# Block products for a second two-unit stage, and a new order of loads before it, in a fused linear-attention and bilinear-FFN kernel

## The chip, the core and the metric

The kernel runs on one core of a Trainium2 chip. The metric is the device time of one execution in microseconds (us), the median of 8 runs. An execution takes a little longer than the span of its instructions in the profile. Engines: TensorE (PE; its weight loads are PEld), VectorE (DVE), ScalarE (ACT), GpSimd (POOL) and SyncE (SP), which only issues DMAs. Each engine works through its own instructions in order.

## The reference

Four batches, eight heads, 768 positions, head size 64, in float32. In blocks of 64 positions, with a decay `lam` for each head:

```python
intra = einsum('bhic,bhjc->bhij', qb, kb) * Dmask     # lam**(i-j), lower triangle
out   = intra @ vb + (qb * lam_pow) @ kv_state
kv_state = lam**64 * kv_state + (kb * rev_pow).T @ vb
```

The heads are then laid side by side, x of 3072 x 512, and a bilinear FFN follows: `(x @ w_a) * (x @ w_b) @ w_out`, with `d_ff` = 1536.

## The kernel before, in words

**Units.** A unit is 128 positions of one batch with all heads: 24 units, six for each batch. For each unit the kernel scales q and k by powers of `lam` (`make_qs`, `make_ks`, line 240; k on VectorE for units below 10, else on GpSimd; q on GpSimd), transposes both (`piece_T`, line 271, on TensorE with a copy by ScalarE, for units 4 and 5; by a DMA from unit 6 on), computes scores (`scores`, 284), masks them on VectorE (`mask`, 307), updates the running state (`kv_update`, 362, copied on VectorE, 387), and forms the output from state and scores (`inter`, `intra`, matmuls of line 324), which ScalarE copies into the transposed x of the FFN (`evac_o`, 347).

**Stages.** The FFN works on groups of units, `GROUPS = (4, 2, 4, 4, 4, 4, 2)`. I call the groups stages 0 to 6. Units 0 to 3 are done by code of their own at the start (lines 720 to 786), and the attention of later units is threaded through the FFN of earlier ones. `PLAN` lists, for each stage, slots and pieces: P (scale q and k, load v, issue further loads), T (transpose), S (scores and masks), V (state), O2 (output of two units), TW (sums of weights), W (stores that were kept back). The FFN code calls `hook(slot)` at fixed places, and the pieces are issued there. An engine meets them in that order.

**Two forms of the FFN.** `ffn` (617) forms, for each of the 12 chunks of 128 hidden columns, a = x @ w_a and b = x @ w_b, four matmuls each (`half`, 430), and their product on VectorE (457). `ffn_seven` (484) gets the four blocks of a and b from seven block products instead of eight, in the manner of Strassen: it splits x in two halves of columns and two of rows, and uses sums of weights (`tw`, four per chunk pair, `w_sums`, 459 to 466, on VectorE) and sums of x (`xs`, `sums`, 468 to 480, on VectorE after the stage's last attention output). `step` (516) issues one product and what follows it: ScalarE takes snapshots of partial sums (513), VectorE and GpSimd add and multiply. The block `c11` is added by VectorE (532) for the chunks that `SUM_ON_VEC` names, else by GpSimd after another snapshot (535); one product is always GpSimd's (545). For a two-unit stage there are three blocks, 21 products of eight matmuls with 128 columns; for four units six blocks, 42 products of four matmuls with 256 columns. The hooks lie among the products:

```python
            if s % 7 == 1 and s < 42:
                hook(2 * (s // 7))
            if s % 7 == 4 and s < 35:
                hook(2 * (s // 7) + 1)
        hook(FC - 1)
```

With three blocks the loop ends after s = 25: slot 6 comes behind the 20th product, slot 7 at s = 25 behind no further one, slot 11 right after it, and the 21st product behind eight matmuls with w_out. `S_GROUPS` names the stages that use this form: 2 to 6. Stages 0 and 1 use `ffn`; stage 0 is special, since the weights arrive during it: it goes in steps of columns (`W_STEPS`), and all matmuls with w_out (line 608) come last, in 24 slots (12 to 35) of two matmuls each.

**Loads.** q and k go through SP's queue: eight loads of 256 KB for units 0 to 3, then two a unit (126). They are issued by `pump` (159), which lets at most three units run ahead. v (128 KB a unit, 256) and the weights (18 loads of 256 KB, 146 and 148) go through GpSimd's queue, which also converts them to bf16. Two holds keep the order. GpSimd first copies an element of a q chunk (`q_here`, 723), and so waits until it is there before it loads v. And SP copies an element of a w_out chunk into `landed` (163), and so waits for that chunk before it goes on: in `pending` (152), q and k of unit 4 wait for w_out's chunk 0, of unit 5 for chunk 3, all later for chunk 5.

Of the kernel before, what the change touches and what calls it, by code (L numbers as in the profile page):

```python
# [22 lines left out]
def _bc(ap, dims):  # L23
# [6 lines left out]
W_STEPS = ((0, 1), (2,), (3,), (4, 5))  # L30
# [7 lines left out]

S_GROUPS = (2, 3, 4, 5, 6)
SUM_ON_VEC = {2: (0, 1, 2, 3, 4), 3: (2, 3, 4), 4: (2, 3, 4), 5: (1, 2, 3, 4), 6: (0, 1, 2)}
PLAN = {
# [10 lines left out]
}  # L54
for _g, _u in ((2, 10), (3, 14), (4, 18)):
# [6 lines left out]
def kernel(  # L62
# [11 lines left out]
    nc = tc.nc  # L74
    B, H, S, D = q.shape
# [5 lines left out]
    NU = B * NB  # L81
    assert sum(GROUPS) == NU and GROUPS[0] == PACK
    KS = d_model // 128
    FC = d_ff // 128
# [45 lines left out]
    wb_sb = singles.tile([128, KS, d_ff], BF16, name="wb_sb")  # L130
    wo_sb = singles.tile([128, FC, d_model], BF16, name="wo_sb")
# [4 lines left out]
    w_off = [sum(W_CHUNKS[:i]) for i in range(len(W_CHUNKS) + 1)]  # L136
# [7 lines left out]
    def load_w(kind, c):  # L144
        if kind == "o":
            nc.gpsimd.dma_start(out=wo_sb[:, 2 * c:2 * c + 2, :], in_=wo_r[:, 2 * c:2 * c + 2, :])
        else:
            nc.gpsimd.dma_start(out=w_part(wa_sb if kind == "a" else wb_sb, c),
                                in_=w_part(wa_r if kind == "a" else wb_r, c))

    n0 = GROUPS[0]
    pending = [("after", 0), ("q", n0), ("k", n0), ("after", 3), ("q", n0 + 1), ("k", n0 + 1), ("after", 5)]
    for u in range(n0 + 2, NU):
        pending += [("q", u), ("k", u)]
    landed = singles.tile([1, 16], BF16, name="landed")
    q_here = singles.tile([128, 1], F32, name="q_here")
    used = {"u": 0}

    def pump():
        while pending:  # L160
            kind, c = pending[0]
            if kind == "after":
                nc.sync.dma_start(out=landed[:, c:c + 1], in_=wo_sb[0:1, 2 * c + 1, 0:1])
            elif c >= used["u"] + 3:
                return
            else:
                load_x(kind, c)
            pending.pop(0)
# [14 lines left out]
    x4 = {}  # L183
# [69 lines left out]
    def make_vb(u):  # L253
        b, nb = divmod(u, NB)
        vb = prep_pool.tile([128, H, D], BF16, name="vb", tag="vb", bufs=8)
        nc.gpsimd.dma_start(out=vb, in_=vr[b, nb])  # L256
        U.setdefault(u, {})["vb"] = vb
# [210 lines left out]
    def sums(u):  # L468
        g = next(i for i in range(len(GROUPS)) if g_u0[i] <= u < g_u0[i] + GROUPS[i])
        if g not in S_GROUPS or u != g_u0[g] + GROUPS[g] - 1:  # L470
            return
# [231 lines left out]
    def scores4(i, ups, ats):  # L703
        kqs = []
        for up, at in zip(ups, ats):
            kq = [ps_bank(f"kq{par}", [128, HP, 128], F32, at=at[par]) for par in range(2)]
            for uu in range(2):
                cols = slice((2 * up + uu) * BLK, (2 * up + uu + 1) * BLK)
                for j in range(2):
                    for par in range(2):  # L710
                        p = slice(64 * par, 64 * par + 64)
                        nc.tensor.matmul(kq[par][:, 2 * uu + j, :],
                                         lhsT=xT4["k"][p, 2 * i + j, cols],
                                         rhs=xT4["q"][p, 2 * i + j, cols],
                                         start=True, stop=True, skip_group_check=True)
            kqs.append(kq)
        for up, kq in zip(ups, kqs):
            ms4[i, up] = mask(kq, split=(i == 1 and up == 1))

    for u in range(n0):  # L720
        U[u] = dict(kn=kn4[:, u], qT=xT4["q"][:, :, u * BLK:(u + 1) * BLK],
                    m=lambda i, hp, u=u: ms4[hp // 2, u // 2][i][:, 2 * (u % 2) + hp % 2, :])
    nc.gpsimd.tensor_copy(q_here, x4["q", 3][:, 0, 0, 0:1])
    for u in range(n0):
        make_vb(u)
    for kind, c in (("a", 0), ("a", 1)):
# [23 lines left out]
    def kv_part(u, hps):  # L750
        for w in range(u + 1):
            kv_mms(sts[u], w, hps, w == 0)

    scores4(1, (0, 1), ((5, 2), (6, 0)))
    for cs in W_STEPS:
        for kind, c in [("a", c) for c in cs] + [("b", c) for c in cs]:
            if (kind, c) not in (("a", 0), ("a", 1)):
                load_w(kind, c)
    for c in range(FC // 2):
        load_w("o", c)  # L760
        if c in (3, 5):
            make_vb(n0 + (c - 3) // 2)
    for u in range(2):
        kv_part(u, (0, 1))
    for u in range(2):
# [21 lines left out]
    bank["held"].clear()  # L787
    used["u"] = n0
    pump()

    for g, n in enumerate(GROUPS):
# [62 lines left out]
```

## Time and profile before

| What | us |
|---|---|
| Median of 8 runs | 224.58 (224.04 to 225.17) |
| The profiled execution | 225.17 |
| Its span | 223.5 |
| Stage 0, a and b parts: from the first to w_out's first matmul | 18.48 to 39.45 |
| Stage 0, w_out with attention of units 4 and 5 between | 39.45 to 54.41 |
| Stage 1: a and b parts, attention of 6 to 9, w_out | 54.41 to 74.70 |
| Stages 2, 3, 4, 5 begin | 74.70, 108.66, 142.06, 175.50 |
| Stage 6 begins | 205.70 |

The page gives busy time for each engine, the span in 40 slices, and the costliest groups of instructions. Of the trace, the timeline lists instructions in order of time: start, duration, engine, line, operation, output and inputs, shape, count, and in square brackets how long the engine had been idle before and what ended that. A window gives busy time of each engine in a stretch, the granted clock of TensorE (1.00 is full), the busy share of the DMA engines, and GB/s.

### The profile page before, as it was taken

Reading aid. Unit: us, or ns where it says so; the run is one execution under the profiler, and the core shown is the slowest. Engines: PE = TensorE matmul, PEld = TensorE weight load, DVE = VectorE, ACT = ScalarE, POOL = GpSimd, SP = SyncE. Lnnn points to the kernel's source line nnn. Section 1 sums busy time; section 2 is a strip of 40 time slices with the busy share of each in tenths; the row PEclk is TensorE's granted clock in tenths of the full one; section 3 lists DMA queues with packets and bytes.
Section 4 is the critical chain, followed back from the end, with each engine's and each line's share of the span. In section 5 each row is a group of like instructions: output and inputs, shape, how many; then the busy total and the mean of one; then the engine's idle time right before and its main releaser. Section 6 shows DMA issues by size and latency. Waiting matters only on the chain.

```text
span 223.5 us, 5209 instructions
## 1 busy us (share of the span) xinstructions
PE 214.1 (96%) x2080; PEld 146.7 (66%) x2099; DVE 146.0 (65%) x250; ACT 99.8 (45%) x182; POOL 117.4 (53%) x131
## 2 busy tenths in 40 slices
PE   7898999989999999999999999999999999999994
PEld 2475444435874688754688754688754688745974
DVE  0991575975696788893678763578763598730760
ACT  2685224018432656324565424566424556332622
POOL 6689352058147569895178993178920144600240
PEclk9999999999999999999999999999999999999999
DMA  4999999989999999999960999500921200012102
GB/s 126 270 130 176 198 205 197 194 186 214 193 206 231 210 240 123 212 332 228 265 167 6 188 211 227 125 4 9 124 58 47 97 1 3 0 47 97 47 3 94
DMA packets 98605, 31.79 MB, mean 142 GB/s; under 512 B 86550, under 2 KB 95638, under 8 KB 98582
## 3 DMA queue, kind: packets, MB, share of 16 engines
q1 hardware_dynamic: 66390, 23.53, 46.5%
q0 software_dynamic: 31904, 7.87, 36.9%
q8 instruction: 16, 0.26, 0.5%
q10 hardware_dynamic: 288, 0.07, 0.1%
q14 instruction: 7, 0.06, 0.1%
HBM read 28.32 MB, written 6.29 MB: 155 GB/s over the span
## 4 chain that ended last, share of the span: by engine, by line
PE 59%; DMA 14%; POOL 13%; DVE 4%; issue 3%; ACT 3%; SPq 1%; POOLq 0%; ACTq 0%
PE op L608 22%; PE m_q L498 13%; DMA wb_sb<-in_moe_w_b_dram 8%; PE m_r L498 7%; POOL ab L545 5%; PE o_ps L324 4%; DMA vb<-in_v_dram 4%; POOL qk L240 3%; PE m_p L498 3%; PE kq L290 3%; DMA k<-in_k_dram 3%; PE a_ps L430 2%; PE b_ps L430 2%; POOL c L535 2%; POOL vb L256 2%
## 5 line engine op out<-in xcount | busy, mean ns | idle before, releaser
L608 PE MATMUL op<-wo_sb,ab 128*128 128x512 bf16 (+2 forms) x295 | 65.7, 362 | 2.0 <-issue 0.8
L545 POOL TENSOR_TENSOR ab<-c,c 128x512 bf16<-128x512 bf16 x27 | 31.4, 1166 | 33.8 <-DVE c L543 33.4
L498 PEld LDWEIGHTS <-tw 128*128 128x128 bf16 x480 | 43.2, 98 | 6.3 <-DVE xs L477 0.3
L608 PEld LDWEIGHTS <-ab 128*128 128x128 bf16 x312 | 27.6, 98 | 27.6 <-POOL ab L545 1.6
L307 DVE TENSOR_TENSOR m<-kq,lotri 128x512 bf16<-128x512 f32 x47 | 29.8, 684 | 6.6 <-PE kq L290 6.1
L498 PE MATMUL m_q<-xs,tw 128*128 128x256 bf16 (+1 forms) x240 | 32.4, 262 | 0.0
L603 ACT COPY o_sb<-op 128x512 f32<-128x512 f32 (+2 forms) x20 | 10.9, 544 | 44.3 <-PE op L608 44.3
L240 POOL TENSOR_TENSOR qk<-qf,lp_q 128x512 bf16<-128x512 f32 x20 | 21.0, 1051 | 17.3 <-DMA qf<-in_q_dram 17.3
L535 POOL TENSOR_TENSOR c<-s 128x512 bf16<-128x512 f32 x9 | 11.4, 1270 | 31.4 <-ACT s L513 31.4
L552 DVE TENSOR_TENSOR ab<-c,m_q 128x512 bf16<-128x512 f32 x27 | 18.6, 687 | 10.6 <-PE m_q L498 8.8
L498 PEld LDWEIGHTS <-wa_sb 128*128 128x128 bf16 x240 | 21.5, 98 | 2.9
L256 POOL DMA_DIRECT2D vb<-in_v_dram x24 | 22.3, 933 | 1.1 <-DMA wa_sb<-in_moe_w_a_dram 0.6
L457 DVE TENSOR_TENSOR ab<-a_sb,b_ps 128x512 bf16<-128x512 bf16 (+1 forms) x24 | 13.1, 551 | 14.1 <-PE b_ps L430 13.9
L513 ACT COPY s<-m_q 128x512 f32<-128x512 f32 x27 | 15.8, 587 | 14.4 <-PE m_q L498 14.1
L543 DVE TENSOR_TENSOR c<-u,m_r 128x512 f32<-128x512 f32 x27 | 18.4, 682 | 5.1 <-ACT u L513 3.2
L532 DVE TENSOR_TENSOR c<-s,m_p 128x512 bf16<-128x512 f32 x18 | 12.4, 687 | 11.1 <-PE m_p L498 11.0
L439 ACT CAST a_sb<-a_ps 128x512 bf16<-128x512 f32 (+1 forms) x24 | 11.4, 479 | 18.1 <-PE a_ps L430 18.1
L430 PE MATMUL a_ps<-xT,wa_sb 128*128 128x256 bf16 (+1 forms) x102 | 18.1, 312 | 1.0 <-DMA wa_sb<-in_moe_w_a_dram 0.9
L549 DVE TENSOR_TENSOR c<-s,m_q 128x512 f32<-128x512 f32 x27 | 18.5, 686 | 0.5
L513 ACT COPY s<-m_r 128x512 f32<-128x512 f32 x27 | 15.9, 588 | 6.5 <-PE m_r L498 6.5
L430 PE MATMUL b_ps<-xT,wb_sb 128*128 128x512 bf16 (+1 forms) x96 | 18.4, 326 | 0.1
L513 ACT COPY u<-m_q 128x512 f32<-128x512 f32 x27 | 16.0, 593 | 5.2 <-PE m_q L498 5.2
(81 smaller groups left out, 290.8 us busy)
## 6 DMA issues: line engine op xcount, KB each, us to landing
qf<-in_q_dram SPq DMA_DIRECT2D x20, 256.0 KB, 4.3
kf<-in_k_dram SPq DMA_DIRECT2D x20, 256.0 KB, 4.9
out_dram<-o_sb SPq DMA_DIRECT2D x17, 256.0 KB, 2.0
vb<-in_v_dram POOLq DMA_DIRECT2D x24, 128.0 KB, 4.8
wa_sb<-in_moe_w_a_dram POOLq DMA_DIRECT2D x6, 256.0 KB, 8.1
wb_sb<-in_moe_w_b_dram POOLq DMA_DIRECT2D x6, 256.0 KB, 8.6
wo_sb<-in_moe_w_out_dram POOLq DMA_DIRECT2D x6, 256.0 KB, 10.2
out_dram<-o_kept SPq DMA_DIRECT2D x6, 256.0 KB, 4.0
```

Source lines behind the costliest of these rows:

```text
L240: eng_of(eng).tensor_mul(dst.rearrange("p (c b) d -> p b c d", b=2), x[:].rearrange("p (b c) d -> p b c d", b=2), lp.rearrange("p (b c) o ...
L256: nc.gpsimd.dma_start(out=vb, in_=vr[b, nb])
L307: nc.vector.tensor_mul(m, kq[i], lotri_bc)
L430: nc.tensor.matmul(ps[:, lo:hi], lhsT=w_sb[:, s, f * 128:(f + 1) * 128], rhs=xT[:, s, lo:hi], start=(s == 0), stop=(s == KS - 1), skip_gro ...
L498: nc.tensor.matmul(ps[:, f, :], lhsT=w(k, f), rhs=x[:, k, :], start=(first and f == 0 and k == 0), stop=True, skip_group_check=True)
L513: nc.scalar.copy(t, ps)
L535: nc.gpsimd.tensor_add(d["c11"], d["s12"][:, 0], d["s12"][:, 1])
L543: nc.vector.tensor_add(c12, d["u2"], d["r"])
L545: nc.gpsimd.tensor_mul(ab[:, nf * i:nf * i + nf, 0:h], d["c11"], c12)
L549: nc.vector.tensor_add(d["c22"], d["s5"], d["q"])
L552: nc.vector.tensor_mul(ab[:, nf * i:nf * i + nf, h:2 * h], d["c22"], d["q"])
L608: nc.tensor.matmul(op[:, lo:hi], lhsT=ab[:, f, t * 128:(t + 1) * 128], rhs=wo_sb[:, f, lo:hi], start=(f == 0), stop=(f == FC - 1))
```

## The change

- Stage 1 uses `ffn_seven` as well (`S_GROUPS`), with all three `c11` on VectorE. The sums of x for it follow the output of units 4 and 5, which moves from slot 34 of stage 0 to slot 31, and with it all that comes before: units 4 and 5 are prepared at slots 15 and 20 instead of 23 and 27.
- The sums of weights, which stage 1 now needs, stand at slots 1, 3, 5, 7, 11 and 18 of stage 0 instead of 4 to 18.
- In stage 1 the attention of units 6 and 7 moves among the products: scores of 6 at slot 6, state of 6 and scores of 7 at slot 7, output of both at slot 11 as before. Some preparations move in stages 0, 1, 3 and 4.
- `SUM_ON_VEC`: in stages 2 to 5 the chunks whose `c11` VectorE adds are others (in 2 and 5 as many as before, in 3 and 4 three as before, now with the last one).
- `pending`: q and k of unit 4 wait for w_b's chunk 3, of unit 5 for w_out's chunk 0, of unit 6 for chunk 3, all later for chunk 5.
- `q_here` copies from q's chunk 1 instead of 3, so GpSimd loads v of units 0 to 3 sooner.
- Two chunks of w_b are issued ahead of a mask that GpSimd does for units 2 and 3, and v of unit 4 is loaded after w_out's chunk 2 instead of 3.

```diff
-S_GROUPS = (2, 3, 4, 5, 6)
-SUM_ON_VEC = {2: (0, 1, 2, 3, 4), 3: (2, 3, 4), 4: (2, 3, 4), 5: (1, 2, 3, 4), 6: (0, 1, 2)}
+S_GROUPS = (1, 2, 3, 4, 5, 6)
+SUM_ON_VEC = {1: (0, 1, 2), 2: (0, 1, 2, 3, 5), 3: (1, 3, 5), 4: (1, 3, 5), 5: (1, 2, 4, 5), 6: (0, 1, 2)}
 PLAN = {
-    0: [(0, "V", 3), (4, "TW", 0), (6, "TW", 1), (9, "TW", 2), (11, "TW", 3), (14, "TW", 4),
-        (18, "TW", 5), (23, "P", 4), (26, "T", 4), (27, "P", 5), (28, "S", 4), (30, "T", 5),
-        (31, "V", 4), (32, "S", 5), (34, "O2", (4, 5)), (35, "P", 6)],
-    1: [(1, "P", 7), (3, "P", 8), (6, "P", 9), (7, "S", 6), (8, "V", 6), (9, "S", 7), (11, "O2", (6, 7)),
+    0: [(0, "V", 3), (1, "TW", 0), (3, "TW", 1), (5, "TW", 2), (7, "TW", 3), (11, "TW", 4),
+        (15, "P", 4), (18, "TW", 5), (19, "T", 4), (20, "P", 5), (22, "S", 4), (25, "T", 5), (26, "V", 4),
+        (27, "P", 6), (28, "S", 5), (31, "O2", (4, 5)), (33, "P", 7)],
+    1: [(2, "P", 8), (4, "P", 9), (6, "S", 6), (7, "V", 6), (7, "S", 7), (11, "O2", (6, 7)),
         (12, "S", 8), (12, "V", 8), (13, "S", 9), (13, "P", 10), (14, "O2", (8, 9)), (15, "P", 11)],
...
-    3: [(6, "P", 18), (9, "P", 19), (13, "P", 20), (16, "P", 21)],
-    4: [(6, "P", 22), (9, "P", 23)],
+    3: [(4, "P", 18), (7, "P", 19), (13, "P", 20), (16, "P", 21)],
+    4: [(4, "P", 22), (7, "P", 23)],
...
-    pending = [("after", 0), ("q", n0), ("k", n0), ("after", 3), ("q", n0 + 1), ("k", n0 + 1), ("after", 5)]
-    for u in range(n0 + 2, NU):
+    pending = [("after", ("b", 3)), ("q", n0), ("k", n0), ("after", ("o", 0)), ("q", n0 + 1), ("k", n0 + 1),
+               ("after", ("o", 3)), ("q", n0 + 2), ("k", n0 + 2), ("after", ("o", 5))]
+    for u in range(n0 + 3, NU):
         pending += [("q", u), ("k", u)]
...
-                nc.sync.dma_start(out=landed[:, c:c + 1], in_=wo_sb[0:1, 2 * c + 1, 0:1])
+                i = used["gates"] = used["gates"] + 1
+                nc.sync.dma_start(out=landed[:, i:i + 1],
+                                  in_=wo_sb[0:1, 2 * c[1] + 1, 0:1] if c[0] == "o" else
+                                  wb_sb[0:1, 3, w_off[c[1]]:w_off[c[1]] + 1])
...
-    nc.gpsimd.tensor_copy(q_here, x4["q", 3][:, 0, 0, 0:1])
+    nc.gpsimd.tensor_copy(q_here, x4["q", 1][:, 0, 0, 0:1])
...
+    w_order = [(kind, c) for cs in W_STEPS for kind in "ab" for c in cs]
+    w_order += [("o", c) for c in range(FC // 2)]
+    for kind, c in w_order[2:4]:
+        load_w(kind, c)
     scores4(1, (0, 1), ((5, 2), (6, 0)))
-    for cs in W_STEPS:
-        for kind, c in [("a", c) for c in cs] + [("b", c) for c in cs]:
-            if (kind, c) not in (("a", 0), ("a", 1)):
-                load_w(kind, c)
-    for c in range(FC // 2):
-        load_w("o", c)
-        if c in (3, 5):
-            make_vb(n0 + (c - 3) // 2)
+    for kind, c in w_order[4:]:
+        load_w(kind, c)
+        if (kind, c) in (("o", 2), ("o", 5)):
+            make_vb(n0 + (c == 5))
```

More of the change, by code (lines that the diff above doesn't have):

```diff
@@ L156 @@
     q_here = singles.tile([128, 1], F32, name="q_here")
-    used = {"u": 0}
+    used = {"u": 0, "gates": 0}
     def pump():
```

## The prediction

> **What bounds the kernel now.** I read the page first, then the timeline of TensorE, then those of VectorE and GpSimd over the same microseconds, then the windows on the DMA.
>
> ```profile
> PE 214.1 (96%) x2080; PEld 146.7 (66%) x2099; DVE 146.0 (65%) x250; ACT 99.8 (45%) x182; POOL 117.4 (53%) x131
> ...
> PEclk9999999999999999999999999999999999999999
> ```
>
> TensorE is busy for 96% of the span at full granted clock. So only two things count: the time of its own instructions, and the few stretches where it stands still. The timeline of TensorE gives the stage borders and those stops:
>
> ```profile
> 18.48 3.65 PE L430 MATMUL a_ps<-xT,wa_sb 128*128 128x256 bf16 x23 [0.88 <-DMA wa_sb<-in_moe_w_a_dram]
> ...
> 39.45 6.64 PE L608 MATMUL op<-wo_sb,ab 128*128 128x512 bf16 x29
> ...
> 47.25 0.40 PE L276 MATMUL tps<-ident,qk 128*128 128x128 bf16 x4 [0.82 <-DVE qk L240]
> ...
> 54.41 0.86 PE L430 MATMUL a_ps<-xT,wa_sb 128*128 128x256 bf16 x4
> 55.11 0.60 PE L430 MATMUL b_ps<-xT,wb_sb 128*128 128x256 bf16 x4
> 55.54 0.60 PE L430 MATMUL a_ps<-xT,wa_sb 128*128 128x256 bf16 x4
> ...
> 74.70 0.60 PE L498 MATMUL m_q<-xT,wa_sb 128*128 128x256 bf16 x4
> ...
> 128.71 1.03 PE L608 MATMUL op<-wo_sb,ab 128*128 128x512 bf16 x4
> 130.04 0.60 PE L608 MATMUL op<-wo_sb,ab 128*128 128x512 bf16 x2 [0.30 <-POOL ab L545]
> ...
> 206.14 0.61 PE L498 MATMUL m_r<-xs,tw 128*128 128x128 bf16 x8
> 206.59 0.61 PE L498 MATMUL m_p<-xT,wa_sb 128*128 128x128 bf16 x8
> ```
>
> Starts, not durations, give the pace, since matmuls overlap. Stage 1 (units 4 and 5) runs from 54.41 to 74.70, 20.29 us; its a and b parts start every 0.437 us. The last stage shows the same two-unit size with seven products: one every 0.45 us. The stop of 0.88 us is the first weight chunk, 0.82 is unit 4's k, and the one at 130.04 is GpSimd.
>
> **Part 1, the products.** Stage 1 loses 24 parts x 0.437 = 10.5 us and gets 21 products x 0.4475 = 9.4 us: -1.1 us of TensorE time, from rows of the same tile sizes.
>
> **Part 2, what stage 1 gets in exchange.** VectorE had 12 products of 0.42 us; it now has four additions or products per block, 12 x 0.68, and four sums of 0.29 (rows of the last stage). That is covered while products run, since VectorE starts one every 0.60 us and a block lasts 3.1. It is not covered at the end. The scores of unit 6, the state of unit 6 and the scores of unit 7 now all stand behind the 20th of 21 products, and the attention output of 6 and 7 (slot 11) follows with nothing between. Counted from the stage's start by the last stage's rows (product 20 at +8.55; its last VectorE addition, late by the two k scalings that lie in this queue, 9.52 to 10.12): VectorE then does two masks, a state copy and two masks, five starts of 0.60, ending at 13.1. TensorE has done scores, state, scores (0.33 + 0.23 + 0.33) by 10.0, waits for the state copy until 12.0, and for the last mask until 13.2; first w_out matmul at 13.5. The rest is 24 matmuls x 0.216, one product 0.45, two scores and a state 0.9, attention output 0.95, some 0.5 of gaps and mask waits: 8.0. Stage 1 lasts 21.5 against 20.29: **+1.2 us**. In the kernel before, unit 6's and 7's scores stood between a and b parts, so this wait is new: about 2.5 us. Even with no VectorE backlog the five operations leave 2.0 (+0.7 for the stage); with the GpSimd operations slowing VectorE's sums as at 74.95 (1.15 instead of 0.42) it is +1.8.
>
> The timeline has no TensorE stop as long as the 2.0 us piece, and the clock stays full throughout. The Trainium skill (TensorE: Matmul & The Clock Gate, "Why this matters for your kernels") says that idle gaps over about 3 us bring the clock to half. By that rule 2.0 is still safe; were it not, its window of 3.4 us at half clock would be an estimated +1.7 us. No row here shows it, and the sum leaves it out.
>
> **Part 3, v and the first weights sooner.** GpSimd waited for the fourth q chunk at 7.73; the second was issued 1.0 us earlier on SP, and chunks land in order some 5 us after issue, so it goes on near 6.3. All of its DMAs (four v at 0.93, then weights) move up by 1.4, and two w_b chunks pass the mask at 14.42, which waits for ScalarE anyway (they end at 13.8). But the k chunks still run until 10.0 in the DMA, and v starts among them: some 330 k packets are left, so k lands 0.3 us later and the weight stream gains 0.9 rather than 1.4. The k scalings have no slack (each starts as its chunk lands), so attention of units 0 to 3 ends at 17.7, not 17.4; w_a lands near 17.5. FFN start: 18.48 to 17.7, **-0.75** (bounds 0 and -1.0).
>
> **Part 4, q and k of units 4 and 5 ahead of w_out, weight sums spread.** The a and b parts stay at 20.97 us: w_a and w_b land 0.7 to 1.8 us ahead of use (from what GpSimd's DMA issues wait for), and q and k start behind w_b's third chunk, when the last a and b chunks are on their way. The sums (1.5 us each) now stand between VectorE's b products; a bank is wanted again seven allocations later, over 2 us away. So w_out starts at 38.7. Without a stop, 48 matmuls, two transposes, two scores, a state and one attention output are 13.1 us against 14.96 now. With stops, k of unit 5 decides:
>
> ```profile
> 41.53 3.44 SPq L126 DMA_DIRECT2D kf<-in_k_dram  x1
> ...
> 48.25 0.73 DVE L240 TENSOR_TENSOR qk<-kf,lp_k 128x512 bf16<-128x512 f32 x1 [1.06 <-DMA kf<-in_k_dram]
> ```
> ```profile
> 40.00:42.00 2.00, 1.95 (x10) 0.88 (x9) 1.97 (x5) 0.00 (x0) 0.00 (x0) 1.00 1.51 165
> 42.00:44.00 2.00, 2.00 (x11) 0.90 (x10) 1.97 (x7) 0.00 (x0) 0.00 (x0) 1.00 1.38 239
> 44.00:46.00 2.00, 2.00 (x10) 0.77 (x8) 1.97 (x4) 0.00 (x0) 1.11 (x1) 1.00 0.50 103
> 46.00:48.00 2.00, 1.18 (x12) 0.75 (x12) 1.19 (x3) 0.32 (x1) 0.61 (x1) 1.00 0.87 199
> ```
>
> The last two columns are DMA share and GB/s. The DMA is full from 9 us to 44, so loads put first only push others back: k of 5 lands at 48.25 after all weights, two v and q, k of 4. What can move it is the stream's start (-0.9) and the hole at 44 to 46, when SP was held in k's issue (103 GB/s against some 220: -1.05). Against it, two queues together moved 165 at 40 to 42 where the weights' queue alone makes 192 (36 to 40): I take +0.5, bounds 0 and +1.9 if the mixture lasts 8 us longer at that loss. So 46.8 (46.3 to 48.2). From there: scaling 0.65, transposes 0.3, ten slots of 0.432, state, scores, output and gaps 1.7: stage 1 starts at k + 6.95 = 53.75, **-0.65** with part 3 in it. Unit 4's k (near 43, by packet counts of 40 to 42) holds its transposes for 1.3 us, which is inside this. The sums of stage 1 have 1.7 us of w_out matmuls over them.
>
> The Trainium skill (DMA: Bandwidth & Descriptors, "Queues, rings and completion order") says that an engine takes turns between its queues packet by packet. The packet records of 40 to 41.5 agree (528 of the one queue, 516 of the other). By the rule q and k advance no faster than the weights' packets, which speaks against this part.
>
> **Part 5, c11 on VectorE for the last block.** In stages 3 and 4 TensorE stands from 129.57 (128.71 + 4 x 0.216) to 130.04 for GpSimd's last product, and the same at 163.5. GpSimd's addition before it (1.27 us) moves to VectorE, which was idle 1.06 us there, and its loads come earlier: the product ends near 129.35, **-0.45 twice = -0.9** (bounds 0 and -0.95). Stages 2 and 5 show no such stop: nothing.
>
> **Sum.** -0.65 + 1.2 - 0.9 = -0.35. The profiled execution took 225.17 us (span 223.5), so 224.8; it is the slowest of the eight runs, whose median is 224.58, and against that: **224.2 us**. By part 4 the sum is (landing of unit 5's k) - 47.15.
>
> **Rivals.** *Loads in time*: no hole and no loss by mixing, so that w_out runs unbroken: stage 1 from 52.3, -2.1 + 1.2 - 0.9 = -1.8, 222.8 us. For: two fewer loads behind w_out. Against: the full DMA. *Loads late, slower*: the mixture costs its full price and k of unit 5 lands at 48.2, +1.05, 225.6. It decides for slower from 47.6 on; for it, the turns between queues and a fourth outstanding load that held SP for 3.44 us; against, the 0.9 us head start. *The new stop halves the clock*: 224.2 + 1.7 = 225.9. *The products are not what they seem*: saving real in the rows, but all stops as priced and part 5 absent: +0.55, 225.1.
>
> **Chances.** About 0.2% (0.45 us) can be told from no change. Forecast 0.38, of which 0.18 lies beyond -0.45; loads in time (also partly) 0.25; loads late 0.27; clock 0.03; part 5 absent 0.07. Faster 0.18 + 0.25 = 0.43, same 0.20, slower 0.37. Range 222.8 to 225.7: it leaves out a tenth or so at either end. The forecast's own range is 223.7 to 224.7.
>
> **What would show it.** FFN start near 17.7; k of unit 5 scaled near 46.8 and stage 1's first product near 53.75; a stop of about 2 us in front of line 324 right after two score groups near 63 to 66, ended by VectorE's line 387 or 307; stage 2's first product 21.5 us after stage 1's; no stop for line 545 in stages 3 and 4. Wrong if that stop is under 1 us, or if stage 1 starts outside 53 to 54.6.

## The result, and the profile after

| | median us | range | ratio to before (95%) |
|---|---|---|---|
| before, timed alongside | 224.82 | 58 runs | |
| after | 226.58 | 225.57 to 228.35, 21 runs | 1.0087 [1.0073, 1.0100] |

The change makes the kernel 0.9% slower. The forecast was 224.2 us and its range ended at 225.7; the result lies above both. The profiled execution of after took 226.06 us, with a span of 224.4 against 223.5. Line numbers in after are four higher (op 612, products 502, scores 294, output 328, mask 311, state copy 391, k and q scaling 244).

The page of after, its row of busy time and its slices of TensorE and of the clock:

```profile
PE 213.1 (95%) x2152; PEld 148.2 (66%) x2171; DVE 148.8 (66%) x254; ACT 100.4 (45%) x179; POOL 121.0 (54%) x134
...
PE   7899999989959999999999999999999999999994
...
PEclk9999999999997999999999999999999999999999
```

TensorE is busy for 1.0 us less, yet the span is longer. The slice with a 5 is new, and the slice after it shows a clock that is not full, which no slice of before does. The timeline of TensorE gives the places:

```profile
46.42 0.40 PE L280 MATMUL tps<-ident,qk 128*128 128x128 bf16 x4 [0.89 <-DVE qk L244]
...
52.65 0.61 PE L502 MATMUL m_q<-xT,wa_sb 128*128 128x128 bf16 x8
53.09 0.61 PE L502 MATMUL m_r<-xs,tw 128*128 128x128 bf16 x8
...
62.14 0.23 PE L294 MATMUL kq<-qkT 64*128 64x128 bf16 x1
62.97 0.38 PE L294 MATMUL kq<-qkT 64*128 64x128 bf16 x7 [0.60 <-DVE ab L556]
63.28 0.40 PE L358 MATMUL kvd<-vb,qk 128*128 128x128 bf16 x4
63.61 0.40 PE L294 MATMUL kq<-qkT 64*128 64x128 bf16 x8
65.96 0.31 PE L328 MATMUL o_ps<-qkT,st 64*64 64x128 bf16 x8 [1.95 <-DVE st L391]
66.20 1.38 PE L328 MATMUL o_ps<-m,vb 128*64 128x128 bf16 x16
...
76.70 0.60 PE L502 MATMUL m_q<-xT,wa_sb 128*128 128x256 bf16 x4
...
128.86 1.24 PE L612 MATMUL op<-wo_sb,ab 128*128 128x512 bf16 x5
129.94 0.60 PE L502 MATMUL m_q<-xT,tw 128*128 128x256 bf16 x4
130.37 1.46 PE L612 MATMUL op<-wo_sb,ab 128*128 128x512 bf16 x6
```

Read off in order: the first score matmul of unit 6 is followed by 0.60 us in which VectorE still reads the bank that the other seven need (a bank is a piece of the memory that TensorE writes its results to; I call this the bank stop); then come 1.95 us in front of the attention output of 6 and 7; then sixteen output matmuls take 1.38 us. At the end of stage 1 sixteen such matmuls take 0.64, and in this place at full clock, with a wait for the last mask among them, 1.01 (experiment 2): the rest is the clock. The last three lines show that the stop in front of line 549's product (0.30 after the first four matmuls, before) is gone.

| stage borders | before | after | difference |
|---|---|---|---|
| first FFN product | 18.48 | 17.25 | -1.23 |
| w_out | 39.45 | 38.22 | -1.23 |
| stage 1 begins | 54.41 | 52.65 | -1.76 |
| stage 1 lasts | 20.29 | 24.05 | +3.76 |
| stage 2 lasts | 33.96 | 33.63 | -0.33 |
| stages 3 to 5 last | 97.04 | 95.85 | -1.19 |
| stage 6 to the end of the span | 17.77 | 18.19 | +0.42 |

The last five rows add up to +0.90, the difference of the two spans. Nearly all that was lost lies in stage 1. The +0.42 lies behind all work: from the last DMA packet to the end of the span after takes 1.76 us, before 1.35. All profiled kernels with the new `pending` show 1.7 to 1.8 us there, all without it 1.3 to 1.4. Why, no run shows. The windows of after over the stop in stage 1 (the number before the last two is the granted clock):

```profile
62.00:64.00 2.00, 1.40 (x24) 0.79 (x21) 2.00 (x4) 0.00 (x0) 1.91 (x3) 1.00 1.58 191
64.00:66.00 2.00, 0.05 (x6) 0.04 (x8) 2.00 (x5) 0.00 (x0) 2.00 (x3) 1.00 1.44 260
66.00:68.00 2.00, 1.94 (x33) 1.37 (x34) 1.27 (x3) 0.97 (x2) 1.98 (x3) 0.64 1.80 193
68.00:70.00 2.00, 1.78 (x5) 0.76 (x5) 0.52 (x1) 0.20 (x1) 2.00 (x3) 0.50 1.28 258
```

While TensorE stands, VectorE is busy 2.00 of 2.00 us: the stop is VectorE's queue. The clock is half from 66.57 to 69.98, 3.413 us by the trace's clock records. One such stretch lowers the mean clock of a run by 0.008. All runs of after show a mean clock of 0.985 to 0.992; of the 101 runs of before timed beside the experiments all show 0.998 to 1.000, save two with 0.992.

### The profile page after: what moved, and what is told of

Same layout as the page of the kernel before. It is cut to its first block, busy times and chain, and to the rows that moved or that the text cites. A ratio compares the mean times of both kernels' runs of the same rounds, so it can differ in the third digit from the quotient of the medians.

```text
span 224.4 us, 5343 instructions
## 1 busy us (share of the span) xinstructions
PE 213.1 (95%) x2152; PEld 148.2 (66%) x2171; DVE 148.8 (66%) x254; ACT 100.4 (45%) x179; POOL 121.0 (54%) x134
## 4 chain that ended last, share of the span: by engine, by line
PE 72%; DMA 13%; DVE 4%; POOL 3%; ACT 2%; issue 2%; SPq 2%; ACTq 0%
PE op L612 24%; PE m_q L502 23%; PE m_r L502 12%; DMA kf<-in_k_dram 6%; PE m_p L502 6%; DMA wo_sb<-in_moe_w_out_dram 5%; PE o_ps L328 4%; DMA k<-in_k_dram 3%; PE kq L294 2%; DVE m L311 2%; POOL wa_sb L148 1%; POOL wb_sb L148 1%; SPq L196 1%; PE kvd L358 1%; ACT o_kept L603 1%
## 5 line engine op out<-in xcount | busy, mean ns | idle before, releaser
L549 POOL TENSOR_TENSOR ab<-c,c 128x512 bf16<-128x512 bf16 x30 | 34.8, 1164 | 42.9 <-DVE c L547 42.0
L502 PEld LDWEIGHTS <-tw 128*128 128x128 bf16 x576 | 49.1, 98 | 6.4 <-issue 0.3
L502 PE MATMUL m_q<-xs,tw 128*128 128x256 bf16 (+1 forms) x288 | 36.1, 255 | 0.2 <-ACT s L517 0.2
L502 PEld LDWEIGHTS <-wa_sb 128*128 128x128 bf16 x288 | 24.5, 98 | 3.1
L547 DVE TENSOR_TENSOR c<-u,m_r 128x512 f32<-128x512 f32 x30 | 20.5, 682 | 5.6 <-ACT u L517 5.6
L553 DVE TENSOR_TENSOR c<-s,m_q 128x512 f32<-128x512 f32 x30 | 20.6, 685 | 0.5
L351 ACT CAST xT<-o_ps 128x512 bf16<-128x512 f32 x22 | 12.0, 588 | 17.4 <-PE o_ps L328 17.1
L502 PE MATMUL m_q<-xT,wa_sb 128*128 128x256 bf16 (+1 forms) x144 | 18.1, 255 | 0.0
L502 PE MATMUL m_p<-xT,wa_sb 128*128 128x256 bf16 (+1 forms) x144 | 18.1, 255 | 0.0
L502 PE MATMUL m_q<-xT,tw 128*128 128x256 bf16 (+1 forms) x144 | 18.1, 255 | 0.0
```

The source lines that it names most:

```text
L351: nc.scalar.copy(dst, src)
L502: nc.tensor.matmul(ps[:, f, :], lhsT=w(k, f), rhs=x[:, k, :], start=(first and f == 0 and k == 0), stop=True, skip_group_check=True)
L547: nc.vector.tensor_add(c12, d["u2"], d["r"])
L549: nc.gpsimd.tensor_mul(ab[:, nf * i:nf * i + nf, 0:h], d["c11"], c12)
L553: nc.vector.tensor_add(d["c22"], d["s5"], d["q"])
```

## The experiments

Two theories. **A**: the stop of 1.95 us and the half clock behind it are the whole cost. **B**: VectorE (and GpSimd) have too much to do throughout stage 1, so filling one stop only moves the wait. Experiments 1 to 4, 7, 10 and 13 take stage 1 apart; 5, 6, 8, 9, 11, 12 and 14 the other parts. The ratios are to the kernel before, timed alongside: 224.64 us for experiments 1, 2, 4 and 5, 225.0 for 3, 6, 7 and 8, 224.64 for 9 to 12, 224.69 for 13 and 14. Medians from different groups are compared by their ratios.

**1. One slot later.** After, with w_out matmuls in the stop:

```diff
-    1: [... (7, "S", 7), (11, "O2", (6, 7)),
+    1: [... (7, "S", 7), (12, "O2", (6, 7)),
```

> The kernel after, with the attention output of units 6 and 7 one slot later in stage 1 (12 instead of 11), so that eight w_out matmuls and the last product stand in front of it and run while VectorE does the masks. Theory A (the stop, and the half clock that follows it, are what costs): both go, stage 1 lasts some 20 us instead of 24.05, the clock is 1.000 up to the end, and the time falls by 3.5 to 4 us to about 222.8. Theory B (VectorE and GpSimd are too full all through stage 1): the wait only moves behind the matmuls or to units 8 and 9, and less than 2 us are won, about 225.

223.61 us, 0.9954 [0.9923, 0.9985], between the two theories; the clock is 0.997 or more in ten of twelve runs. Stage 1 lasts 20.96. The timeline of TensorE keeps two other stops:

```profile
62.87 0.38 PE L294 MATMUL kq<-qkT 64*128 64x128 bf16 x7 [0.59 <-DVE ab L556]
...
68.26 0.38 PE L358 MATMUL kvd<-vb,qk 128*128 128x128 bf16 x4 [0.45 <-DVE st L391]
```

One slot is worth 3 us. But with the stop filled, stage 1 is still 0.67 longer than the plain form's 20.29: A explains most, B the rest.

**2. and 3. Idle matmuls in the stop.** After, with ten, and then five, matmuls on zeros of 512 columns in front of the output of 6 and 7, which only keep TensorE busy:

```diff
+        if us == (6, 7):
+            o67 = U[6]["o"][0]
+            for _ in range(10):
+                nc.tensor.matmul(_bc(o67, [o67.ap[0], [1, 512]]), lhsT=idle_sb[:, :128],
+                                 rhs=idle_sb, start=True, stop=True, skip_group_check=True)
```

> The kernel after, with ten dummy matmuls of 512 columns put in front of the attention output of units 6 and 7; they write zeros into a bank that is overwritten next, and run while TensorE would stop. The stop in the computation stays as long. If the half clock comes from TensorE's idleness there: the clock stays 1.000, and 1.7 us are won (one stretch of 3.4 us at half speed), 224.8. If the half clock comes from something else in stage 1 (load of the stage as a whole): no gain, 226.6 or slightly more.

225.29 us, 1.0019 [0.9993, 1.0046], 1.3 less than after (1.7 expected); stage 1 lasts 22.74, clock 1.000 in the profile and 0.997 or more in all twelve runs.

> The kernel after with five idle matmuls instead of ten in front of the attention output of units 6 and 7. They fill some 1.1 us of the stop of 1.95, so that about 0.9 is left beside the 0.6 and 0.3 us stops ahead of it. If what halves the clock is the length of the single stop or the share of the preceding 3.4 us that TensorE is busy (43% in the kernel after), this keeps the clock at 1.000 and gives what ten gave, 225.3. If the sum of the stops in this neighbourhood were enough whatever fills them, the clock shows a half-speed window again and the time is 226.5.

225.41 us, 1.0007 [0.9979, 1.0036]; stage 1 again 22.74, clock 0.997 or more. With five, the timeline of TensorE shows this left of the stop:

```profile
64.05 1.25 PE L412 MATMUL o_ps<-idle_sb 128*128 128x512 bf16 x5
66.08 0.31 PE L328 MATMUL o_ps<-qkT,st 64*64 64x128 bf16 x8 [0.77 <-DVE st L391]
```

So at full clock stage 1 lasts 22.74, and the half clock adds 24.05 - 22.74 = 1.3 us. The prediction had 21.5: another 1.2 us is not the clock's.

**4. Stage 1 in its plain form.** After, without part 1 and 2:

```diff
-S_GROUPS = (1, 2, 3, 4, 5, 6)
+S_GROUPS = (2, 3, 4, 5, 6)
-    1: [(2, "P", 8), (4, "P", 9), (6, "S", 6), (7, "V", 6), (7, "S", 7), ...
+    1: [(3, "P", 8), (6, "P", 9), (7, "S", 6), (8, "V", 6), (9, "S", 7), ...
```

> The kernel after, with stage 1 in plain form as before (its slots of before too, except that units 8 and 9 are prepared at slots 3 and 6); loads, weight sums, GpSimd's order and the other stages as after. Theory A: stage 1 begins near 52.6, lasts 20.3 as before, and stages 3 and 4 keep their gain: 224.8 - 1.8 - 0.9 = 222.1. If the gain before stage 1 is given back later (by loads that come late for units 8 and up), stage 1 or 2 shows new waits and the time is 223 to 224.

222.93 us, 0.9917 [0.9889, 0.9945], between the two expectations; stage 1 starts at 52.80 and lasts 20.03 with no stop at all. The seven products are a loss of 0.9 us of stage 1 even in experiment 1: the work saved on TensorE is smaller than the waits it buys on VectorE.

**5. Part 5 alone.** Before, with

```diff
-SUM_ON_VEC = {2: (0, 1, 2, 3, 4), 3: (2, 3, 4), 4: (2, 3, 4), 5: (1, 2, 3, 4), 6: (0, 1, 2)}
+SUM_ON_VEC = {2: (0, 1, 2, 3, 5), 3: (1, 3, 5), 4: (1, 3, 5), 5: (1, 2, 4, 5), 6: (0, 1, 2)}
-    3: [(6, "P", 18), (9, "P", 19), ...     4: [(6, "P", 22), (9, "P", 23)],
+    3: [(4, "P", 18), (7, "P", 19), ...     4: [(4, "P", 22), (7, "P", 23)],
```

> The kernel before, with only the choice of chunks whose c11 VectorE adds in stages 2 to 5, and the earlier preparation of two units in stages 3 and 4, taken from the change. My step: the stops of 0.47 us in stages 3 and 4 go and nothing comes instead: -0.9, 223.9. The rival: VectorE or the loads are late instead, no gain, 224.8.

223.55 us, 0.9938 [0.9909, 0.9967]; from stage 3's start to the end of the span 113.63 instead of 114.81. Part 5 is worth 1.2 (predicted 0.9).

**6. Part 3 alone.** Before, with

```diff
-    nc.gpsimd.tensor_copy(q_here, x4["q", 3][:, 0, 0, 0:1])
+    nc.gpsimd.tensor_copy(q_here, x4["q", 1][:, 0, 0, 0:1])
...
+    for c in (0, 1):
+        load_w("b", c)
     scores4(1, (0, 1), ((5, 2), (6, 0)))
```

> The kernel before with part 3 alone: v of unit 0 waits for the second q chunk, and two w_b chunks are issued ahead of GpSimd's mask. The prediction's part 3 by itself: first FFN product near 17.3 to 17.7 (17.25 in the kernel after) and the whole gain kept, 0.75 us: about 223.9. Rival: the gain is given back in front of the transposes of units 4 and 5, whose k still comes behind the weights in the same number of bytes; then stage 1 starts within 0.3 us of the kernel before's (54.41 in its trace), the stop in front of those transposes grows by what the FFN start won, and the time is 224.4 to 224.8.

226.29 us, 1.0044 [1.0013, 1.0075]: slower. Both expectations fail: the first FFN product comes at 17.33, but stage 1 starts at 56.08, 1.7 us later than before. The timeline of its TensorE:

```profile
47.65 0.40 PE L276 MATMUL tps<-ident,qk 128*128 128x128 bf16 x4 [2.50 <-DVE qk L240]
```

And of its VectorE just before that:

```profile
44.33 1.15 DVE L464 TENSOR_TENSOR tw<-wb_sb,tw 128x512 bf16<-128x512 bf16 x1
45.40 0.41 DVE L465 TENSOR_TENSOR tw<-wb_sb 128x512 bf16<-128x512 bf16 x1
45.74 1.26 DVE L466 TENSOR_TENSOR tw<-wa_sb,tw 128x512 bf16<-128x512 bf16 x1
46.92 1.28 DVE L240 TENSOR_TENSOR qk<-kf,lp_k 128x512 bf16<-128x512 f32 x2
```

Both k are scaled back to back, with no wait for a load: they stood behind the weight sums on VectorE, some of which take 1.2 us instead of 0.42. TensorE reached w_out 1.15 us sooner (38.30), but VectorE ended the sums no sooner, so that TensorE only waits longer. The stop of 2.50 is followed by half clock in this profile; seven of the twelve runs show a clock of 0.992. Those took 226.9 us in the median, the five at full clock 225.4: the half clock is 1.5 us.

**7. Two k scalings on GpSimd.** Experiment 1, with k of units 8 and 9 scaled there (`n0` is 4):

```diff
-        make_ks(u, "dve" if u < n0 + 6 else "pool")
+        make_ks(u, "dve" if u < n0 + 4 else "pool")
```

> The kernel after with the attention output of 6 and 7 one slot later, as in the first experiment (223.6), and with the two k scalings of units 8 and 9 moved from VectorE to GpSimd. Theory B (VectorE is too full in stage 1, and its k scalings of 1.12 and 1.27 us are the largest pieces): VectorE gains about 2.4 us before the masks, the stop in front of the scores of unit 6 (0.59) goes, stage 1 drops from 20.96 to about 20.0 and the time is 222.5 to 222.9. Rival: GpSimd becomes the late one; its q and k scalings (1.5 us each) hold its products and additions, stops named GpSimd appear in stage 1, and the time is 223.6 or more.

224.69 us, 0.9976 [0.9948, 1.0004]; the interval overlaps that of experiment 1, but nothing is gained, and stage 1 lasts 21.42 instead of 20.96. The rival holds: the bank stop goes, but GpSimd ends q of unit 9 at 63.84 instead of 62.52, and its scores then wait for their transpose, as the timeline of TensorE shows:

```profile
70.19 0.40 PE L294 MATMUL kq<-qkT 64*128 64x128 bf16 x8 [1.30 <-DMA qkT<-qk]
```

**8. Part 4 alone.** Before, with the new `pending` and its holds, w_out's place for v of unit 4, and the new row 0 of `PLAN`, as in the diff of the change; stage 1 plain:

```diff
-    1: [(1, "P", 7), (3, "P", 8), ...
+    1: [(3, "P", 8), ...
```

> The kernel before with part 4 alone: q and k of units 4 and 5 issued ahead of w_out behind their gates, the weight sums spread over the first FFN step, stage 1 as before, v and the first weights as before. Read from the kernel after, part 4 is worth what its stage 1 start gained (1.76 us) less what part 3 alone gives: if part 3 alone gives nothing at stage 1's start, this gives all of it, and stage 1 starts near 53; the time is 223.0 to 223.8. If parts 3 and 4 need each other (the hole in the loads goes only when GpSimd's weights are early), this gives under 0.6 us at stage 1's start and 224.2 or more. The prediction's own sum gives part 4 alone +0.1: 224.7.

227.78 us, 1.0101 [1.0059, 1.0143]. Worse than any price given. Without the head start of part 3 the loads are too late for the earlier slots. The timeline of TensorE:

```profile
47.98 0.40 PE L280 MATMUL tps<-ident,qk 128*128 128x128 bf16 x4 [1.55 <-POOL qk L244]
49.57 0.40 PE L280 MATMUL tps<-ident,qk 128*128 128x128 bf16 x4 [1.20 <-DVE qk L244]
```

The two scalings of unit 5 that it waits for, on GpSimd (q) and VectorE (k), each wait for their load:

```profile
46.88 1.04 POOL L244 TENSOR_TENSOR qk<-qf,lp_q 128x512 bf16<-128x512 f32 x1 [7.04 <-DMA qf<-in_q_dram]
...
48.83 0.69 DVE L244 TENSOR_TENSOR qk<-kf,lp_k 128x512 bf16<-128x512 f32 x1 [4.54 <-DMA kf<-in_k_dram]
```

Stage 1 starts at 55.80. Three of the six runs show a clock of 0.992 (227.85 to 228.36); the three at full clock took 226.75 to 227.71. So parts 3 and 4 each cost time alone, and gain it together (experiment 4 against 5, timed alongside: 222.93 and 223.55).

**9. Unit 5 later.** Experiment 4 ("the third" in the text below), with

```diff
-        ... (25, "T", 5), (26, "V", 4), (27, "P", 6), (28, "S", 5), (31, "O2", (4, 5)), ...
+        ... (25, "V", 4), (27, "T", 5), (28, "P", 6), (30, "S", 5), (32, "O2", (4, 5)), ...
```

> The third experiment's kernel (parts 3, 4 and 5, stage 1 as before; 222.9) with the state of unit 4 one slot sooner and the transposes of unit 5 two slots later, behind four more w_out matmuls, and what follows them a slot or two later. Its stop of 0.96 in front of those transposes, which wait for the k of unit 5, should go: expected 0.86 less, 222.0 to 222.2, stage 1 from 51.9. Rival: the work only changes places and the wait moves to the scores or the attention output behind it; then 222.7 or more.

222.60 us, 0.9907 [0.9881, 0.9932], between the two expectations and not to be told from experiment 4. Stage 1 starts at 51.95, as expected, but lasts 20.97: the wait moved to two transposes by DMA, in the timeline of TensorE:

```profile
61.73 0.40 PE L294 MATMUL kq<-qkT 64*128 64x128 bf16 x8 [0.22 <-DMA qkT<-qk]
...
68.85 0.40 PE L294 MATMUL kq<-qkT 64*128 64x128 bf16 x8 [0.59 <-DMA qkT<-qk]
```

**10. One k scaling on GpSimd.** As experiment 7, for unit 8 alone:

```diff
-        make_ks(u, "dve" if u < n0 + 6 else "pool")
+        make_ks(u, "dve" if u < n0 + 6 and u != n0 + 4 else "pool")
```

> The kernel after with the attention output of 6 and 7 one slot later (223.6) and the k scaling of unit 8 alone on GpSimd. The trace of the first experiment shows that scaling at 1.12 us on VectorE with GpSimd's q scaling at 1.48 beside it. If theory B's amount is right, VectorE has 1.12 us more, the q scaling falls to 1.04, so GpSimd ends its queue no later, and the stop of 0.59 in front of the scores of unit 6 goes without the stop of 1.30 that moving two scalings gave: stage 1 of 20.2 to 20.4, 223.0. Even so seven products would only equal the plain form here (20.03). Rival: the bank stop stays since the last products, not the queue behind them, hold VectorE: 223.6.

225.66 us, 1.0042 [1.0016, 1.0067]; expectation and rival both miss. VectorE gained 1.1 us on unit 8 and lost 1.8 on unit 9. The timeline of VectorE:

```profile
60.24 3.08 DVE L244 TENSOR_TENSOR qk<-kf,lp_k 128x512 bf16<-128x512 f32 x1
```

And of GpSimd:

```profile
60.60 1.18 POOL L549 TENSOR_TENSOR ab<-c,c 128x512 bf16<-128x512 bf16 x1
61.73 1.04 POOL L244 TENSOR_TENSOR qk<-qf,lp_q 128x512 bf16<-128x512 f32 x1
```

A scaling of 0.68 us lasts until 0.55 us after GpSimd's second operation has ended (62.77). The stop in front of the scores of unit 6 grows to 2.14 and the clock halves (in seven of twelve runs; 226.1 us in the median against 224.8).

**11. Part 3 with the spread of the weight sums, loads as before.** Experiment 6, with

```diff
-    0: [(0, "V", 3), (4, "TW", 0), (6, "TW", 1), (9, "TW", 2), (11, "TW", 3), (14, "TW", 4),
+    0: [(0, "V", 3), (1, "TW", 0), (3, "TW", 1), (5, "TW", 2), (7, "TW", 3), (11, "TW", 4),
```

> Part 3 alone (226.3) with the weight sums spread over the first FFN step as in the kernel after, and nothing else of part 4: q and k of units 4 and 5 come in the order of the kernel before. Its own trace says that the k scaling of unit 4 stood behind weight sums on VectorE until 46.92, 14 us after its load was issued. If VectorE and not the load is what then holds the transposes of unit 4, the stop of 2.50 goes, with it the half clock, the scaling starts at 43 to 44 and stage 1 near 52.5: 223.3 to 224.0. Rival: the loads hold it; k of unit 4 is scaled after 45.5 with an idle time ended by the DMA, and the time is 225 or more.

222.78 us, 0.9914 [0.9893, 0.9934], better than expected: 3.5 us less than experiment 6 by the medians, 2.9 by the ratios. Stage 1 starts at 52.19. VectorE was what held the transposes.

**12. The same with part 5**, the diff of experiment 5 added.

> The kernel of the run before this one with part 5 too (measured alone at -1.4 by its median, -1.1 by its stages). If the parts add up: 222.0 to 222.9, no slower than parts 3, 4 and 5 with the loads ahead of w_out (222.9), which would mean that the order of the loads is worth nothing and the spread of the weight sums is all that part 4 needs. If the order of the loads matters, 223.4 or more.

**221.64 us, 0.9864 [0.9840, 0.9887]** (four runs), better than expected: the fastest version of this study, faster than both kernels. Its timeline of TensorE has both transposes of unit 4 with no stop before them:

```profile
44.69 0.61 PE L276 MATMUL tps<-ident,qk 128*128 128x128 bf16 x8
```

Its VectorE, with k of units 4 and 5:

```profile
42.87 0.68 DVE L240 TENSOR_TENSOR qk<-kf,lp_k 128x512 bf16<-128x512 f32 x1
44.45 0.74 DVE L240 TENSOR_TENSOR qk<-kf,lp_k 128x512 bf16<-128x512 f32 x1 [0.90 <-DMA kf<-in_k_dram]
```

And its SP, where k of unit 5 is issued:

```profile
37.76 3.34 SPq L126 DMA_DIRECT2D kf<-in_k_dram  x1
```

The same issue on SP in the kernel after:

```profile
32.86 3.05 SPq L126 DMA_DIRECT2D kf<-in_k_dram  x1
```

And the scaling that waits for it on VectorE there:

```profile
45.67 0.69 DVE L244 TENSOR_TENSOR qk<-kf,lp_k 128x512 bf16<-128x512 f32 x1 [2.96 <-DMA kf<-in_k_dram]
```

Unit 5's k, issued at 32.86 among the weights, lands at 45.67; issued at 37.76 behind more of them, at 44.45. With the sums spread, there are all four cases of its landing: 47.69 with neither part 3 nor the new order (experiment 14), 48.83 with the new order alone (8), 44.45 with part 3 alone (12), 45.67 with both (after). So part 3 brings this load 3.2 us sooner, and the new order makes it 1.1 to 1.2 later, whichever way they are paired. The whole time says the same: experiment 9 has the new order and took 222.60, timed beside 221.64 here. Some 0.4 of these 0.96 us is the longer end of the span that comes with the new `pending`, and the earlier slots, which were not tried without the new order, have a part too. Of part 4 only the spread of the sums is needed.

**13. No q scaling beside the k scaling.** After; q of units 8 and 9 is copied by ScalarE and its scaling left out.

```diff
-        make_qs(u, "pool")
+        if u in (n0 + 4, n0 + 5):
+            nc.scalar.copy(U[u]["qk"][:, 0].rearrange("p (c b) d -> p b c d", b=2),
+                           raw.pop((u, "q"))[:].rearrange("p (b c) d -> p b c d", b=2))
+        else:
+            make_qs(u, "pool")
```

> The kernel after; q of units 8 and 9 is copied by ScalarE in stage 1 and its scaling left out, so that GpSimd computes nothing beside VectorE's k scalings of these units. If the two engines get in each other's way there, the k scalings take 0.68 us each instead of 1.12 and 1.28, VectorE ends its masks 1.0 us sooner, the stop of 1.95 falls to about 1.3 and the bank stop of 0.6 goes, the clock stays at 1.000, and stage 1 lasts 21.0 to 21.6 as the prediction's working has it: 223.3 to 224.2. Rival: the queue is late for its length alone; the k scalings or what follows them stay as late, a stop of over 1.7 us is left, and the time is 225 or more.

226.45 us, 1.0080 [1.0049, 1.0111]: no change, so the q scalings are not what slows the k scalings. The k scaling of unit 8 takes 1.12 us as in after, of unit 9 1.28, with no q scaling there. What GpSimd has in that place is line 549's product (here line 553). The timeline of VectorE:

```profile
60.08 1.12 DVE L244 TENSOR_TENSOR qk<-kf,lp_k 128x512 bf16<-128x512 f32 x1
...
63.51 1.28 DVE L244 TENSOR_TENSOR qk<-kf,lp_k 128x512 bf16<-128x512 f32 x1
```

And of GpSimd:

```profile
59.49 1.16 POOL L553 TENSOR_TENSOR ab<-c,c 128x512 bf16<-128x512 bf16 x1 [7.16 <-DVE c L551]
...
63.08 1.15 POOL L553 TENSOR_TENSOR ab<-c,c 128x512 bf16<-128x512 bf16 x1 [1.54 <-DVE c L551]
```

The product ends at 60.65, the scaling at 61.20; the next at 64.23 and 64.79. The pairs of after fit likewise, on VectorE:

```profile
57.00 1.12 DVE L244 TENSOR_TENSOR qk<-kf,lp_k 128x512 bf16<-128x512 f32 x1
...
60.43 1.28 DVE L244 TENSOR_TENSOR qk<-kf,lp_k 128x512 bf16<-128x512 f32 x1
```

And on GpSimd:

```profile
56.41 1.16 POOL L549 TENSOR_TENSOR ab<-c,c 128x512 bf16<-128x512 bf16 x1 [5.83 <-DVE c L547]
57.54 1.48 POOL L244 TENSOR_TENSOR qk<-qf,lp_q 128x512 bf16<-128x512 f32 x1
...
60.01 1.16 POOL L549 TENSOR_TENSOR ab<-c,c 128x512 bf16<-128x512 bf16 x1
```

In each the scaling ends 0.54 to 0.56 us after GpSimd's product: it waits for the whole of it and then runs. The q scaling is here the next in line: it starts at 57.54, before the k scaling's end at 58.12, and lasts 1.48 instead of 1.04.

The other profiles settle it. All sixteen together have 93 k scalings on VectorE behind the start phase (after 25 us). 21 of them start while an operation of GpSimd on two inputs is running, be it the product or a q scaling: every one ends 0.55 us after that operation does. Of the other 72, 71 take 0.68 or 0.69 us, and one is the 3.08 of experiment 10. In the plain stage 1 of before, without the product, units 8 and 9 take 0.69 and 0.70. And in experiment 4 a q scaling holds the k scaling of unit 8 just so; on VectorE:

```profile
56.90 1.51 DVE L244 TENSOR_TENSOR qk<-kf,lp_k 128x512 bf16<-128x512 f32 x1
```

And on GpSimd:

```profile
56.82 1.03 POOL L244 TENSOR_TENSOR qk<-qf,lp_q 128x512 bf16<-128x512 f32 x1 [3.51 <-DMA qf<-in_q_dram]
```

So what slows a k scaling is whatever GpSimd has begun before it; in after that is the product.

**14. The spread of the weight sums alone**: the diff of experiment 11 in the kernel before.

> The kernel before with the weight sums spread over the first FFN step and nothing else. In its trace the k scaling of unit 4 starts at 46.51 as the last weight sum ends, with no wait for its load, so its load came sooner by an unknown amount; that of unit 5 waited for its load until 48.25. If the spread works by itself, the stop of 0.82 goes and the one of 0.4 to 0.5 behind it stays or grows: 0.3 to 0.8 less, 223.8 to 224.3. Rival: the load lands only just before 46.5, or the wait moves to unit 5's k, and the time is within 0.2 of the kernel before; then the spread is worth something only where the loads are sooner (with v sooner it gave 3.5 of 226.3).

224.31 us, 0.9972 [0.9953, 0.9991], at the edge of the expectation. The stop in front of the transposes falls from 0.82 to 0.18, and VectorE, in its timeline, now waits for the load:

```profile
45.89 0.69 DVE L240 TENSOR_TENSOR qk<-kf,lp_k 128x512 bf16<-128x512 f32 x1 [2.40 <-DMA kf<-in_k_dram]
```

The four cases side by side, as ratios to before: neither 1, spread alone 0.9972, v sooner alone 1.0044, both 0.9914.

## Why the prediction was wrong

- **The failed step is part 2, first by a term that it put at nothing.** It said of its 2.0 us stop that it "is still safe", left the half clock out of the sum and gave it a chance of 0.03. The clock halved in every run of after. That rival's price, +1.7, is near what was measured (1.3 from experiments 2 and 3, 1.5 within experiment 6, 1.4 within 10).
- **The same step mis-sized stage 1 at full clock**: 21.5, measured 22.74. The term is VectorE's queue. The last addition ahead of the masks was to start 9.52 us into the stage, "late by the two k scalings"; but in the last stage of before, which has no k scalings, it starts at 9.51 (the VectorE row below, less the stage's start at 205.70), so they were not in that figure.

```profile
215.21 0.68 DVE L549 TENSOR_TENSOR c<-s,m_q 128x512 f32<-128x512 f32 x1
```

  In after it starts at 10.78 (63.43 on VectorE), in experiment 7, where both k scalings are gone from this queue, at 9.86. So 0.9 of the 1.26 goes with the k scalings: they took 1.05 and 1.21 instead of 0.60 from start to start, because GpSimd's product was running. The prediction priced a slowing by GpSimd only for the sums of x, at the stage's start. The bank stop of 0.60 ahead of the scores was not foreseen; it comes from the same late queue, since it is gone in experiment 7.
- **The size of the stop was right in part by luck.** The piece of 2.0 measured 1.95, but both its ends came 1.3 us later than said (64.01 and 65.96 instead of 62.65 and 64.65), and the "about 2.5" in all match 0.60 + 1.95 only because the bank stop stands where the prediction had a wait for the last mask.
- **The lock.** The Trainium skill (SBUF — State Buffer, "SBUF: two separate sides") says that VectorE and GpSimd share a pair of ports as an exclusive lock: whichever starts first holds it for the instruction, and the other is fully blocked; VectorE needs it for two inputs in SBUF. The runs agree but for one (1.12 and 1.28 instead of 0.68, while two masks at 64.03, which read PSUM, take 1.28 together beside a product of GpSimd, as elsewhere; the one is the 3.08 of experiment 10). The prediction should have drawn GpSimd's operations over VectorE's queue for all of stage 1.
- **Part 1 was right.** The first 20 products start 0.45 us apart but for a stop of 0.22 at 54.37 and smaller ones, the 24 parts 0.437. It does not show in the time: the saving went into waits for VectorE.
- **Part 3 as an edit by itself was wrong.** "-0.75" for the FFN start; -1.23 measured, since GpSimd issued v and the first weights 2.1 us sooner (8.38 to 6.25, 12.03 to 9.90), not 1.4. (The start differs between executions too: 17.68 in the profile of experiment 5, which leaves it as before.) But alone the edit loses 1.3 us by the median (experiment 6): the weight sums on VectorE and GpSimd's part in them were taken as free.
- **Part 4.** The rule "stage 1 starts at k + 6.95" held: 45.67 + 6.95 = 52.62, measured 52.65, and in experiments 4 and 8 likewise (52.77 for 52.80, 55.78 for 55.80). But k landed 1.1 us sooner than said, and 52.65 lies outside the 53 to 54.6 that the prediction had set itself. That the miss is no larger is luck: of its terms for the landing, the sooner stream was worth 3.0 to 3.2 us and not 0.9, and the new order cost 1.1 to 1.2 where the hole less the mixing was to gain 0.55. The doubt that the prediction raised itself, that q and k put among the weights advance no faster, was right and should have had the weight: experiment 12 lands unit 5's k 1.2 us sooner without the new order.
- **Part 5 was right**: 0.9 predicted, 1.2 measured alone and in after, and no stop for line 549 is left.
- **The sum** had errors of both signs: stage 1's start came 1.1 us better than said, stage 1 itself 2.55 worse, stages 2 to 5 0.6 better, and the end of the span 0.42 worse. The profiled run took 226.06 where the sum for it was 224.8.

## What to carry to other kernels

Ahead of a stop that a change creates, lay out the other engines' queues beside it: what saves work on the bound engine is paid for where the helper engines meet, and a saving of 1.1 us was lost there more than three times over. When a stage must wait, put independent matmuls into the wait: one slot was worth 3 us here, more than the edit itself could gain. And test parts of a change in pairs as well as alone: one that loses 1.3 us alone and the useful half of one that loses 2.8 gave, with part 5, the best version.

## What was not expected of the hardware

**The clock.** All changes of the granted clock within a trace lie whole multiples of 3.413 us apart, so a run has a fixed grid. The share of each grid window in which TensorE was busy, for the windows with a long stop, and the clock of the next window:

| run | window from (us) | TensorE busy | next clock |
|---|---|---|---|
| experiment 6 | 44.99 | 0.27 | 0.5 |
| experiment 13 | 65.65 | 0.31 | 0.5 |
| experiment 10 | 61.91 | 0.37 | 0.5 |
| after | 63.16 | 0.41 | 0.5 |
| experiment 13 | 45.17 | 0.47 | 0.5 |
| experiment 7 | 67.19 | 0.49 | 1.0 |
| experiment 8 | 45.11 | 0.50 | 1.0 |
| experiment 7 | 43.30 | 0.68 | 1.0 |

In these profiles a window that is 0.47 busy or less is followed by one at half clock, and one that is 0.49 busy or more is not. (Busy is by the profile, which models the ends of matmuls.) No single long stop is needed: a stop of 1.95 us was enough, and so were these two in experiment 13 with four matmuls between:

```profile
46.32 0.40 PE L284 MATMUL tps<-ident,qk 128*128 128x128 bf16 x4 [0.60 <-POOL qk L244]
47.92 0.40 PE L284 MATMUL tps<-ident,qk 128*128 128x128 bf16 x4 [1.20 <-DVE qk L244]
```

The Trainium skill (TensorE: Matmul & The Clock Gate, "What's actually happening") has the free-running window of 3413 ns, which agrees, but lets the clock fall after an idle window; here windows that were 0.27 to 0.47 busy had the same effect.

The grid lies differently in each profile, so the same stop can fall into one window or be split over two, and a kernel can have two times: 225.4 and 226.9 in experiment 6. As an estimate, I laid the grid in every position over the traces and counted those in which some window is under 0.48 busy: 0.69 for experiment 6, 0.59 for 10, 0.65 for 8, where seven of twelve, seven of twelve and three of six runs show a half clock; none for before and experiments 1 to 4 and 7. For after it gives 0.73, but all 21 runs lost a window, so either the grid did not lie evenly over those runs or something else counts too; which, no run shows. Nor does it explain the single runs of before and of experiments 1, 4 and 7 with a clock of 0.992 or less, which have no profile.

**GpSimd and VectorE.** One scaling of 0.68 us took 3.08 behind two operations of GpSimd that started after it (experiment 10); why the lock went to the later ones stays open. A DMA issue of GpSimd ended just before them, 0.34 us into the scaling; but in after a k scaling at 48.11 that stands the same way to a DMA issue (until 48.53) and a q scaling (from 48.55) took 0.68.
